# Decode attention with a 48-KB place for the second half of each head's values, and transposes one chunk ahead of the scores

## The chip, the cores and the metric

One core of a Trainium2 chip. The time is that of one execution on the device in microseconds; a kernel is run several times and the median is quoted. The profile is of one execution; its own clock, used in the timelines, starts with the span.

## The reference, cut to what matters

One token passes a pre-norm attention block over a cache and then a small ReLU MLP. There are 32 heads (numbered 0 to 31), a cache of 32768 positions, and 192 values per position and head, all in bf16:

```python
q = (layernorm(x) @ wq)                          # x: 1 x 640, 32 heads of 192
scores = einsum("bhqd,bhkd->bhqk", q, k_cache) * 192 ** -0.5
o = einsum("bhqk,bhkd->bhqd", softmax(scores), v_cache)
h = x + o @ wo
out = h + relu(layernorm(h) @ w1) @ w2           # 640 -> 1536 -> 640
```

Keys and values are 2 x 32 x 32768 x 192 x 2 bytes = 805 MB of the 825 MB that are read. There is one query, so each byte is used once.

## The kernel before

A head is cut into 8 chunks of 32 columns of 128 positions (1 column: one position in each partition). Of each chunk TensorE transposes 20 or 16 columns of keys (line "tp" of the profile), ScalarE copies them out of PSUM ("kT"), TensorE makes their scores ("sp"), and VectorE multiplies and sums the other 12 or 16 columns by itself ("pr", "sc"). ScalarE takes the exponentials of both ("pB", "pA"), and TensorE adds up the values with them ("o_ps"); I call that the value sums of a chunk. The end of a head is a sum of the denominators ("den"), a scaling on VectorE ("o_pair"), a turn of the row into a column on TensorE ("mm<-wide,o_pair") and a copy of it by VectorE ("oT").

GpSimd passes each landing of a load on to the engines (a "relay"), so in the profile a wait "<-POOLq" of TensorE or VectorE is a wait for a load. Keys of half a head are one load of 48-KB rows (K0, K1). Values are four loads of 24-KB rows (V0 to V3) through two places:

```python
    kt = [sbuf(f"kt{i}", [P, JK * Dh], bf16, 512) for i in range(NK)]      # 2 x 48 KB a partition
    vt = [sbuf(f"vt{i}", [P, JL * Dh], bf16, 512) for i in range(NV)]      # 2 x 24 KB
    ...
        for h in range(LAST):                       # the DMA queue, in order; LAST = 31
            keys(h, 0)
            if h > 0:
                vals(h - 1, NL - 1)                 # V3 of the head before
            vals(h, 0)
            keys(h, 1)
            vals(h, 1)
            vals(h, 2)
    ...
    SUMS = ((), (-2,), (-1,), (0, 1), (), (2,), (3,), (4, 5))    # value sums beside chunk c; below 0: of the head before
    def pe_head(g, h, turn=None):
        for c in range(NC):
            transposes(g, h, c)
            ...                                     # den, value sums of SUMS[c]
            scores_pe(g, h, c)
            if c == 3 and h > 0:
                o_turn(g, h - 1)
    ...
    def dve_head(g, h):
        for c in range(len(chunks(h))):
            scores_dve(g, h, c)
            if c == 0 and h > 0:
                den_rec(g, h - 1)
            if c == 2 and h > 0:
                o_scale(g, h - 1)
            if c == 3 and h > 0:
                o_turned(g, h - 1)
```

Heads 1 to 30 run in a loop on each engine. Head 31 is written out apart: its keys and values come in smaller loads and its chunks end with small ones, so that little work is left when the last bytes land. Behind it come w1 and w2 and the MLP.

The softmax here doesn't subtract the row's maximum and nothing guards it: scores larger than these inputs give would overflow.

## Time and profile before

| | before |
|---|---|
| median time | 1920.2 us (3 runs, 1919.48 to 1921.22) |
| span of the profile | 1918.7 us |
| share of the DMA queue's packets | 99.8% |
| VectorE, TensorE busy | 81%, 81% |
| last byte of w2 (packet records) | 1913.6 us |
| output's store issued | 1915.3 us |

The DMA engines are the bound: 39 of the 40 slices show 9 and the last one 8. The prediction shows the lines for it. To them I add those of the end, which it did not look at. They are from the timeline of before (start, length, engine, line, operation, and in brackets the idle time just before it and what ended that):

```profile
start us, us, engine line op out<-in xcount [idle before <-releaser]
...
1821.54 2.56 DVE L688 TENSOR_TENSOR pr<-kt,qb 128x2304 f32<-128x2304 bf16 x1 [2.48 <-POOLq L325]
...
1842.41 3.35 DVE L691 TENSOR_REDUCE sc<-pr 128x16 f32<-128x3072 f32 x1
...
1847.60 2.56 DVE L688 TENSOR_TENSOR pr<-kt,qb 128x2304 f32<-128x2304 bf16 x1 [1.84 <-ACT qb L630]
...
1895.51 1.75 DVE L691 TENSOR_REDUCE sc<-pr 128x8 f32<-128x1536 f32 x1
...
1913.09 1.24 PE L368 MATMUL attT<-h1T,w_s 128*128 128x1 bf16 x30 [0.52 <-DMA w_s<-in_B_w_dram]
...
1915.30 0.36 SPq L230 DMA_DIRECT2D out_dram<-y_row  x1
```

VectorE waits for the second half of head 30's keys until 1821.5 us, ends that head at 1845.8, begins head 31 at 1847.6 and ends its last scores at 1897.3. The MLP's second product waits 0.52 us for w2, so the end hangs on the bytes, but only just: the compute behind head 31 arrives half a microsecond ahead of them.

### The profile page before, as it was taken

The page shows a single profiled execution, that of the slowest core. Times are in us where ns is not written, and L with a number is a line of the kernel's source. Part 1 is how long each engine was busy: PE and PEld are TensorE (multiplying, and loading weights), DVE is VectorE, ACT ScalarE, POOL GpSimd, SP SyncE. Part 2 cuts the span into 40 slices and gives each one's busy share as a digit, 9 for nine tenths or more (in the row PEclk, how much of TensorE's full clock was granted, in tenths as well). Part 3 has the DMA queues.
Part 4 walks back from the last instruction along what each step waited for, and adds up shares of the span by engine and source line. Part 5 has one row for each costly group of instructions (what it writes and reads, how often), then busy time and mean ns, then how long its engine had stood idle before and what let it go on. Part 6 is the DMA issues. An engine that isn't in the chain of part 4 may idle for free.

```text
span 1918.7 us, 36168 instructions
## 1 busy us (share of the span) xinstructions
PE 1560.2 (81%) x15909; PEld 1099.7 (57%) x15909; DVE 1560.0 (81%) x732; ACT 957.9 (50%) x2000; POOL 1.0 (0%) x6
## 2 busy tenths in 40 slices
PE   7787787887877978878878778778788787887887
PEld 7555565555555655655555556556555565565554
DVE  2897787887878978888888879878788787897895
ACT  2554454454554544544545545445445454454463
POOL 0000000000000000000000000000000000000000
PEclk9888888878888878789898888888798888878899
DMA  9999999999999999999999999999999999999998
GB/s 409 429 430 429 432 437 428 434 436 429 436 436 429 435 431 431 438 429 434 436 430 437 433 429 435 430 434 438 428 434 437 427 440 430 431 438 428 434 430 355
DMA packets 34098, 825.29 MB, mean 430 GB/s; under 512 B 3611, under 2 KB 5148, under 8 KB 8604
## 3 DMA queue, kind: packets, MB, share of 16 engines
q1 hardware_dynamic: 34074, 824.98, 99.8%
q8 instruction: 15, 0.25, 0.0%
q14 instruction: 7, 0.06, 0.0%
q10 hardware_dynamic: 2, 0.00, 0.0%
HBM read 824.97 MB, written 0.00 MB: 430 GB/s over the span
## 4 chain that ended last, share of the span: by engine, by line
DMA 55%; PE 30%; DVE 8%; ACT 5%; SPq 1%; issue 1%; POOLq 0%; DVEq 0%; ACTq 0%
DMA kt<-in_A_k_cache_dram 52%; PE o_ps L368 17%; PE tp L387 9%; ACT kT L608 5%; DVE pr L688 4%; DVE sc L691 4%; PE sp L368 3%; DMA vt<-in_A_v_cache_dram 2%; SPq L230 1%; DMA w_s<-in_B_w_dram 1%; PE attT L368 1%; PE mm L368 0%; DMA kt<-in_A_wq_dram 0%; DVEq L65 0%; POOLq L350 0%
## 5 line engine op out<-in xcount | busy, mean ns | idle before, releaser
L688 DVE TENSOR_TENSOR pr<-kt,qb 128x2304 f32<-128x2304 bf16 (+2 forms) x257 | 755.9, 2941 | 299.4 <-POOLq L325 271.2
L608 ACT COPY kT<-tp 128x1024 bf16<-128x1024 bf16 (+1 forms) x899 | 817.7, 989 | 301.2 <-PE tp L387 299.4
L387 PE MATMUL tp<-ident_f,kt 128*128 128x128 f32 x3459 | 580.3, 335 | 238.5 <-POOLq L350 235.7
L691 DVE TENSOR_REDUCE sc<-pr 128x12 f32<-128x2304 f32 (+2 forms) x257 | 755.3, 2939 | 8.9
L387 PEld LDWEIGHTS tp<-ident_f,kt 128*128 128x128 f32 x3459 | 505.2, 175 | 245.6 <-POOLq L350 241.0
L368 PE MATMUL o_ps<-vt,pB 128*2 128x384 bf16 x2286 | 461.9, 352 | 9.0 <-POOLq L350 8.3
L614 ACT ACTIVATE pB<-sp 128x20 bf16<-128x20 f32 (+2 forms) x258 | 48.0, 186 | 569.4 <-PE sp L368 569.4
L368 PE MATMUL o_ps<-vt,pA 128*2 128x384 bf16 x1778 | 330.6, 326 | 0.0
L368 PEld LDWEIGHTS o_ps<-vt,pB 128*2 128x2 bf16 x2286 | 188.0, 88 | 235.5 <-issue 94.5
L368 PE MATMUL sp<-qm,kT 128*128 128x2 bf16 x6918 | 214.3, 164 | 98.4 <-ACT kT L608 96.9
L368 PEld LDWEIGHTS sp<-qm,kT 128*128 128x128 bf16 x6918 | 192.4, 98 | 177.7 <-ACT kT L608 134.5
L368 PEld LDWEIGHTS o_ps<-vt,pA 128*2 128x2 bf16 x1778 | 150.0, 84 | 142.4 <-issue 4.1
L623 ACT ACTIVATE pA<-sc 128x12 bf16<-128x12 f32 (+2 forms) x257 | 53.5, 208 | 39.9 <-DVEq L65 38.9
L614 ACT ACTIVATION_READ_ACCUMULATOR pB<-sp 128x1 f32 x258 | 50.2, 195 | 0.0
L623 ACT ACTIVATION_READ_ACCUMULATOR pA<-sc 128x1 f32 x257 | 48.9, 190 | 0.0
L702 DVE TENSOR_SCALAR o_pair<-o_ps,rec 2x384 bf16<-2x384 f32 x32 | 19.4, 605 | 6.3 <-PE o_ps L368 1.7
L368 PE MATMUL o_ps<-xn_ln,kt 128*96 128x1 bf16 (+1 forms) x316 | 22.4, 208 | 2.6 <-DMA kt<-in_A_wq_dram 2.6
L368 PEld LDWEIGHTS o_ps<-xn_ln,kt 128*96 128x96 bf16 (+1 forms) x316 | 22.2, 175 | 2.7 <-issue 2.6
L368 PE MATMUL attT<-oT,wo_s 128*128 128x1 bf16 x465 | 16.3, 164 | 0.3 <-DVE oT L712 0.3
L712 DVE TENSOR_SCALAR oT<-mm,odd 128x3 bf16<-128x3 f32 x32 | 7.1, 223 | 10.8 <-PE mm L368 8.3
L368 PEld LDWEIGHTS mm<-dsums,ones_mat 128*128 128x128 f32 x64 | 15.4, 295 | 0.3 <-issue 0.3
L696 DVE TENSOR_REDUCE rec<-mm 128x1 f32<-128x20 f32 x32 | 5.7, 179 | 12.0 <-PE mm L368 7.5
(69 smaller groups left out, 151.6 us busy)
## 6 DMA issues: line engine op xcount, KB each, us to landing
vt<-in_A_v_cache_dram SPq DMA_DIRECT2D x126, 3072.0 KB, 19.1
kt<-in_A_k_cache_dram SPq DMA_DIRECT2D x62, 6144.0 KB, 32.6
kt<-in_A_k_cache_dram SPq DMA_DIRECT2D x3, 3072.0 KB, 20.2
wo_s<-in_A_wo_dram SPq DMA_DIRECT2D x16, 480.0 KB, 9.5
kt<-in_A_wq_dram SPq DMA_DIRECT2D x4, 1536.0 KB, 10.8
vt<-in_A_v_cache_dram SPq DMA_DIRECT2D x2, 1536.0 KB, 16.4
kt<-in_A_k_cache_dram SPq DMA_DIRECT2D x1, 1920.0 KB, 28.3
kt<-in_A_v_cache_dram SPq DMA_DIRECT2D x2, 960.0 KB, 21.1
```

The lines of the kernel that those rows point to most:

```text
L230: g.do(lambda: nc.sync.dma_start(out=dst, in_=src), sem, label, by=16)
L368: return lambda: pe.matmul(o, lhsT=w, rhs=r, **kw)
L387: calls.append(lambda b=b, o=o: pe.transpose(out=dst[:, b, :], in_=src[:, o:o + 2 * P].bitcast(f32), identity=ident_f[:]))
L608: g.do(lambda: act.copy(out=kT[c % 2][:, b0:b0 + nb, :], in_=src[:, 0:nb, :].bitcast(bf16)), "act_pe", ("cp", h, c, k))
L614: g.do(lambda: act.activation(out=pB[c % NB][:, 0:jp], in_=sp[:, 0:jp], func=F.Exp, scale=SCALE, accum_out=dsums[:, 2 * c + 1:2 * c + 2]), ...
L623: g.do(lambda: act.activation(out=pA[c % NB][:, 0:jd], in_=sc[c % NC][:, 0:jd], func=F.Exp, scale=SCALE, accum_out=dsums[:, 2 * c:2 * c + ...
L688: g.chain(lambda: dve.tensor_tensor(out=pr[:, 0:j1 - j0, :], in0=src[:, (off + j0) * Dh:(off + j1) * Dh].rearrange("p (j d) -> p j d", d=D ...
L691: g.chain(lambda: dve.reduce_sum(out=sc[c % NC][:, j0:j1], in_=pr[:, 0:j1 - j0, :], axis=X), "dve")
L696: g.chain(lambda: dve.reduce_sum(out=rec[:, 0:1], in_=mm[:, 0:2 * NCM], axis=X), "dve")
L702: g.do(lambda: dve.tensor_scalar_mul(out=o_pair[:, :, 1, :], in0=o_ps[0:2, 0:2 * Dh].rearrange("q (i d) -> q i d", i=2), scalar1=rec[0:2, ...
L712: g.do(lambda: dve.tensor_scalar_mul(out=oT[:], in0=mm[:, 0:3], scalar1=odd[:]), "dve_pe", ("oTc", h))
```

## The change

The intent: fewer and longer rows on a DMA queue that is always full, and a head that ends within itself. The diff, cut to its core (left out: names of semaphores, asserts, the matching order of the relays, places for all 8 chunks' exponentials instead of 5, and ScalarE's order, which now copies a chunk's keys before it takes the exponentials of the chunk before):

```diff
-    vt = [sbuf(f"vt{i}", [P, JL * Dh], bf16, 512) for i in range(NV)]
+    va = sbuf("va", [P, JK * Dh], bf16, 512)          # 48 KB: second half
+    vb = sbuf("vb", [P, JL * Dh], bf16, 512)          # 24 KB: first half, twice
...
-    w2_s = sbuf("w2_s", [P, FT, D], bf16, 512)
+    w2_s = kt[0][:, JL * Dh:JL * Dh + FT * D].rearrange("p (f n) -> p f n", n=D)
...
         for h in range(LAST):
             keys(h, 0)
-            if h > 0:
-                vals(h - 1, NL - 1)
             vals(h, 0)
             keys(h, 1)
-            vals(h, 1)
-            vals(h, 2)
+            for ld in ((2, 1) if h == 0 else (1, 2)):
+                vals(h, ld)                           # 2 is the whole second half
...                                                   # head 31: K0, K1, V0, K2, V1, ... (was K0, V3 of 30, K1, V0, K2, V1, ...)
-    SUMS = ((), (-2,), (-1,), (0, 1), (), (2,), (3,), (4, 5))
+    SUMS = ((), (), (0,), (1,), (), (), (2, 3), (4,), (5, 6, 7))
+    SUMS_0 = ((), (), (0,), (1,), (), (), (4,), (5,), (6, 7, 2, 3))
...
-        for c in range(NC):
-            transposes(g, h, c)
+        for c in range(NC + 1):
+            if c < NC and c != 4:
+                transposes(g, h, c)
...
-            scores_pe(g, h, c)
-            if c == 3 and h > 0:
+            if c > 0:
+                scores_pe(g, h, c - 1)
+            if c == 4:
+                transposes(g, h, 4)
+            if c == 2 and h > 0:
                 o_turn(g, h - 1)
...                                                   # head 31 on TensorE
+        transposes(g, h, 2)
+        values(g, h, 0)
         scores_pe(g, h, 1)
-        ...
+        o_turn(g, h - 1)
...                                                   # VectorE, all heads
             if c == 0 and h > 0:
                 den_rec(g, h - 1)
-            if c == 2 and h > 0:
                 o_scale(g, h - 1)
-            if c == 3 and h > 0:
+            if c == 1 and h > 0:
                 o_turned(g, h - 1)
```

More of the change, by code (lines that the diff above doesn't have):

```diff
@@ L114 @@
     NC = 2 * NL
-    NV = 2
-    NB = 5
+    NB = NC
     LAST = H - 1
     assert Sk % (P * JK) == 0 and NK == 2 and NL == 4 and 2 * Dh == 3 * P and H % 2 == 0 and HE == 3 * P // 4 and DT == 5 and H >= 4
-    full = [(c // 4, (c % 4) * J, J, JPS[c % 2], c // 2, (c % 2) * J) for c in range(NC)]
+    full = [(c // 4, (c % 4) * J, J, JPS[c % 2]) + ((c // 2, (c % 2) * J) if c < 4 else (2, (c - 4) * J)) for c in range(NC)]
     ENDJ = (40, 16, 8)
@@ L198 @@
     mm = psum("mm", [P, 512])
-    wq_c = [kt[1][:, c * H * Dh:(c + 1) * H * Dh] for c in range(DT - 1)] + [vt[1][:, 0:H * Dh]]
+    wq_c = [kt[1][:, c * H * Dh:(c + 1) * H * Dh] for c in range(DT - 1)] + [va[:, 0:H * Dh]]
     assert (DT - 1) * H * Dh == JK * Dh and H * Dh <= JL * Dh
@@ L205 @@
             3: kt[1][:, 64 * Dh:104 * Dh], 4: kt[1][:, 104 * Dh:120 * Dh], 5: kt[1][:, 120 * Dh:128 * Dh]}
-    v_at = {3: kt[0][:, 0:40 * Dh], 4: kt[0][:, 40 * Dh:56 * Dh], 5: kt[0][:, 56 * Dh:64 * Dh]}
-    w1_s = kt[0][:, 64 * Dh:64 * Dh + DT * Dff].rearrange("p (c n) -> p c n", n=Dff)
-    w2_s = sbuf("w2_s", [P, FT, D], bf16, 512)
-    assert DT * Dff <= JL * Dh
+    v_at = {0: vb[:], 1: va[:, 0:JL * Dh], 2: va[:, JL * Dh:2 * JL * Dh],
+            3: vb[:, 0:40 * Dh], 4: vb[:, 40 * Dh:56 * Dh], 5: vb[:, 56 * Dh:64 * Dh]}
+    w1_s = kt[0][:, 0:DT * Dff].rearrange("p (c n) -> p c n", n=Dff)
+    w2_s = kt[0][:, JL * Dh:JL * Dh + FT * D].rearrange("p (f n) -> p f n", n=D)
+    assert DT * Dff <= JL * Dh and FT * D <= JL * Dh
     W2_CUTS = (0, FT // 2, FT - 2, FT)
@@ L215, in v_tile @@
     def v_tile(h, ld):
-        return v_at[ld] if h == LAST and ld in v_at else vt[ld % NV][:]
+        return v_at[ld] if h == LAST else (vb, vb, va)[ld][:]
     names = ["pool_pe", "act_pe", "dve_pe", "act_dve", "dve_act", "dve", "dve_row", "pe_dve", "pool_row", "pool_dve", "pool_act", "pe_act", "pe", "dve_sp"]
-    names += [f"dk{i}" for i in range(NK)] + [f"dv{i}" for i in range(NV)] + ["dwo", "dx", "dout"] + [f"dwq{i}" for i in range(5)]
-    names += [f"dke{i}" for i in range(4)] + ["dvh"] + [f"dve{i}" for i in range(4)] + ["dw1"] + [f"dw2_{i}" for i in range(3)]
+    names += [f"dk{i}" for i in range(NK)] + ["dva", "dvb"] + ["dwo", "dx", "dout"] + [f"dwq{i}" for i in range(5)]
+    names += [f"dke{i}" for i in range(4)] + ["dvh0", "dvh1"] + [f"dve{i}" for i in range(4)] + ["dw1"] + [f"dw2_{i}" for i in range(3)]
     sems = {n: nc.alloc_semaphore(n) for n in names}
@@ L236, in keys @@
             if h > 0:
-                g.wait("PV", h - 1, 2 if h == 1 and ld == 0 else 4 * ld + 1)
+                if ld == 0:
+                    g.wait("PV", h - 1, 4 if h == 1 else 2)
+                else:
+                    g.wait("PV", h - 1, 5)
                 g.wait("scs", h - 1, 4 * ld + 3)
@@ L243, in vals @@
         def vals(h, ld):
-            if ld == 1 and h == LAST:
-                g.wait("vfree")
-            elif ld == 1 and h > 0:
-                g.wait("PV", h, 0)
-            elif ld > 1:
-                g.wait("PV", h, 2 * ld - 3)
-            elif h > 0:
-                g.wait("PV", h - 1, 5)
-            if h < LAST:
-                src = rows(v_hd, h, P * JK * (ld // 2), JK)[:, (ld % 2) * JL * Dh:(ld % 2 + 1) * JL * Dh]
-            else:
-                src = rows(v_hd, h, P * JL * ld, JL)
-            load(vt[ld % NV][:], src, f"dv{ld % NV}", "v", h, ld)
+            if ld == 1:
+                g.wait("PV", h, 1)
+            elif h > 0:
+                g.wait("PV", h - 1, 3 if ld == 0 else NC - 1)
+            src = rows(v_hd, h, P * JK * (ld // 2), JK)
+            if ld < 2:
+                src = src[:, ld * JL * Dh:(ld + 1) * JL * Dh]
+            load((vb, vb, va)[ld][:], src, "dva" if ld == 2 else "dvb", "v", h, ld)
         for c in range(DT):
@@ L275, in end_keys, with end_values @@
             load(k_at[i], rows(k_hd, LAST, k0, jl), sem, "k", LAST, i)
-        for ld in range(NL - 1):
-            if ld != 1:
-                g.wait("PV", LAST - 1, 2 * ld + 1)
-                g.wait("scs", LAST - 1, 2 * ld + 3)
-            end_keys(ld, P * JL * ld, JL, ("dk0", "dke0", "dk1")[ld])
-            if ld == 0:
-                vals(LAST - 1, NL - 1)
-            else:
-                vals(LAST, ld - 1)
+        def end_values(ld, c0, c1, sem, *label):
+            load(v_at[ld][:, c0:c1], rows(v_hd, LAST, P * JL * ld, JL)[:, c0:c1], sem, *label)
+        g.wait("PV", LAST - 1, 2)
+        g.wait("scs", LAST - 1, 3)
+        end_keys(0, 0, JL, "dk0")
+        end_keys(1, P * JL, JL, "dke0")
+        g.wait("PV", LAST - 1, 3)
+        end_values(0, 0, JL * Dh, "dvb", "v", LAST, 0)
+        g.wait("PV", LAST - 1, 5)
+        g.wait("scs", LAST - 1, NC - 1)
+        end_keys(2, 2 * P * JL, JL, "dk1")
+        g.wait("PV", LAST - 1, NC - 1)
+        end_values(1, 0, JL * Dh, "dva", "v", LAST, 1)
         k0 = P * JL * (NL - 1)
@@ L292, in dma_program @@
             k0 += P * jl
-        g.wait("PV", LAST, 1)
-        src = rows(v_hd, LAST, P * JL * (NL - 2), JL)
-        n = J * Dh
-        load(vt[0][:, 0:n], src[:, 0:n], "dv0", "v", LAST, NL - 2)
-        load(vt[0][:, n:2 * n], src[:, n:2 * n], "dvh", "vh")
+        for i in range(2):
+            end_values(2, i * J * Dh, (i + 1) * J * Dh, f"dvh{i}", "vh", i)
         i = 0
@@ L329, in pool_program @@
             key(h, 0)
-            if h > 0:
-                relay(g, "v", h - 1, NL - 1)
             relay(g, "v", h, 0)
             key(h, 1)
-            relay(g, "v", h, 1)
-            relay(g, "v", h, 2)
+            for ld in ((2, 1) if h == 0 else (1, 2)):
+                relay(g, "v", h, ld)
             relay(g, "W", h)
-        for ld in range(NL - 1):
-            key(LAST, ld)
-            if ld == 0:
-                relay(g, "v", LAST - 1, NL - 1)
-            else:
-                relay(g, "v", LAST, ld - 1)
-        relay(g, "v", LAST, NL - 2)
+        key(LAST, 0)
+        key(LAST, 1)
+        relay(g, "v", LAST, 0)
+        key(LAST, 2)
+        relay(g, "v", LAST, 1)
     def relay(g, *label):
@@ L426, in values @@
             g.wait("vc", h, c)
+        elif h == LAST and ld == 2:
+            g.wait("vh", c - 4)
         elif off == 0:
             g.wait("at", "v", h, ld)
-        if h == LAST and c == 5:
-            g.wait("vh")
         g.wait("ep", h, c)
@@ L444, in values @@
                               stop=(c == len(chunks(h)) - 1 and i == len(order) - 1), skip_group_check=True))
-        pe_group(g, calls, ("PV", h, c), "pe_dve" if h < LAST and c == NC - 1 else "pe")
+        pe_group(g, calls, ("PV", h, c), "pe")
     def den_mm(g, h):
@@ L500, in q_spread @@
         pe_group(g, calls, ("qs", h), "pe_act")
-    SUMS = ((), (-2,), (-1,), (0, 1), (), (2,), (3,), (4, 5))
+    SUMS = ((), (), (0,), (1,), (), (), (2, 3), (4,), (5, 6, 7))
+    SUMS_0 = ((), (), (0,), (1,), (), (), (4,), (5,), (6, 7, 2, 3))
     def pe_head(g, h, turn=None):
-        for c in range(NC):
-            transposes(g, h, c)
+        for c in range(NC + 1):
+            if c < NC and c != 4:
+                transposes(g, h, c)
             if c == 0 and h > 0:
                 den_mm(g, h - 1)
-            for d in (SUMS[c] if h > 0 or c > 5 else ((), (0,), (1,), (), (2,), ())[c]):
-                if d >= 0:
+            for d in (SUMS if h > 0 else SUMS_0)[c]:
+                if c < NC:
                     values(g, h, d)
-                elif h > 0:
-                    values(g, h - 1, NC + d)
-            scores_pe(g, h, c)
-            if c == 3 and h > 0:
+            if c > 0:
[3 more added lines that the diff above has]
+            if c == 2 and h > 0:
                 o_turn(g, h - 1)
@@ L521, in pe_head @@
                 q_spread(g, h + 1, turn)
+        for d in (SUMS if h > 0 else SUMS_0)[NC]:
+            values(g, h, d)
     def pe_norm(g):
@@ L546, in pe_end @@
         scores_pe(g, h, 0)
-        values(g, h - 1, NC - 2)
-        values(g, h - 1, NC - 1)
-        pe_group(g, [mmul(attT[0:1, 500:501], ident_b[0:1, 0:1], zero5[0:1, 0:1], start=False, stop=True,
-                          skip_group_check=True)], ("vfree",))
+        transposes(g, h, 2)
+        values(g, h, 0)
         scores_pe(g, h, 1)
-        transposes(g, h, 2)
+        o_turn(g, h - 1)
         transposes(g, h, 3)
+        values(g, h, 1)
         scores_pe(g, h, 2)
-        values(g, h, 0)
+        transposes(g, h, 4)
         scores_pe(g, h, 3)
-        o_turn(g, h - 1)
-        for c in (4, 5):
-            transposes(g, h, c)
-            values(g, h, c - 3)
-            scores_pe(g, h, c)
+        transposes(g, h, 5)
+        values(g, h, 2)
+        scores_pe(g, h, 4)
         transposes(g, h, 6)
         values(g, h, 3)
+        scores_pe(g, h, 5)
         transposes(g, h, 7)
@@ L646, in act_head @@
         q_wide(g, h)
-        for c in range(NC if h < LAST else NC - 2):
-            copies(g, h, c)
-            exp_pe(g, h, c)
-            exp_dve(g, h, c)
+        n = len(chunks(h))
+        for c in range(n):
+            if c == 4 and h < LAST:
+                exp_pe(g, h, 3)
+                exp_dve(g, h, 3)
+                copies(g, h, 4)
+                continue
+            copies(g, h, c)
+            if c > 0:
+                exp_pe(g, h, c - 1)
+                exp_dve(g, h, c - 1)
+        exp_pe(g, h, n - 1)
+        exp_dve(g, h, n - 1)
     def act_end(g):
         act_head(g, LAST)
-        h = LAST
-        copies(g, h, NC - 2)
-        for c in range(NC - 1, NCM):
-            copies(g, h, c)
-            exp_pe(g, h, c - 1)
-            exp_dve(g, h, c - 1)
-        exp_pe(g, h, NCM - 1)
-        exp_dve(g, h, NCM - 1)
         act_norm(g, "ln2")
@@ L699, in o_scale @@
     def o_scale(g, h):
-        g.wait("PV", h, len(chunks(h)) - 1)
+        if h == LAST:
+            g.wait("PV", h, NCM - 1)
         g.wait("rec", h)
```

## The prediction

> **What bounds the kernel now.** I read the page from the top: engine shares, slices, DMA queues.
>
> ```profile
> span 1918.7 us, 36168 instructions
> PE 1560.2 (81%) x15909; PEld 1099.7 (57%) x15909; DVE 1560.0 (81%) x732; ACT 957.9 (50%) x2000; POOL 1.0 (0%) x6
> ...
> DMA  9999999999999999999999999999999999999998
> ...
> DMA packets 34098, 825.29 MB, mean 430 GB/s; under 512 B 3611, under 2 KB 5148, under 8 KB 8604
> ...
> q1 hardware_dynamic: 34074, 824.98, 99.8%
> ```
>
> The 16 DMA engines have no hole in any slice and one queue fills 99.8% of the span, while TensorE and VectorE idle for a fifth of it. 825 MB must be read whatever the order. Next, the busy time by window over the middle of the run, and the DMA queue's own waits:
>
> ```profile
> core 0: us, PE busy (x) PEld busy (x) DVE busy (x) ACT busy (x) POOL busy (x), PEclk, DMA share, GB/s
> ...
> 600.00:1800.00 1200.00, 977.55 (x9887) 687.77 (x9886) 994.39 (x450) 607.77 (x1270) 0.00 (x0) 0.84 1.00 433
> ```
>
> ```profile
> engine line waited for: us in total, times, longest us
> SPq L230 <- PE o_ps L368: 1593.1, 126, 28.0
> ```
>
> The DMA share is 1.00. The issuing queue waits nearly always, and for TensorE's value sums (o_ps) that free a buffer. Such a wait costs nothing while an earlier load still moves. So the kernel is bound by moving bytes, and the question is twofold: does the change make the bytes move faster, and does any of its new waits let the engines run dry.
>
> **How fast a packet moves.** The page counts one packet per row, so a 24-KB row is one packet and a 48-KB row is one. Their durations in the trace's packet records hardly vary: 1280 B 55 ns, 3072 B 121, 12288 B 460, 24576 B 912 (16512 packets), 49152 B 1815 (7936 packets), a semaphore's 4 B 9. From the two large sizes: 1815 - 912 = 903 ns for 24576 B, so 912 - 903 = 9 ns are fixed per packet, and the 4-B packet agrees.
>
> **The Trainium skill.** "DMA: Bandwidth & Descriptors", section "Where 436 GB/s comes from", puts the ceiling of the core's ports at 435.2 GB/s; the trace has 433, so a large gain is not to be had. The same page, "Why small descriptors are slow (HBM only)", names a fixed overhead of about 3 cycles per packet; the trace agrees that there is one, and I use its 9 ns. The same page, "Latency and other measured facts", gives some 600 ns to the first byte; the one load here that met a drying queue was issued at 115.6 us and its first packet started at 117.0, so I use 1.35 us. "TensorE: Matmul & The Clock Gate", "The HAM clock gate", has TensorE at half clock after an idle window of about 3.4 us; the trace agrees: fifteen transposes take 1.84 us, or 3.46 after a wait.
>
> **The change part by part.**
>
> 1. Packets. In each of 31 heads two value loads of 128 24-KB rows become one of 128 48-KB rows: 128 packets fewer, and 16 semaphore packets. (128 + 16) x 9 ns / 16 engines = 0.081 us a head, 2.5 us in all. DMA is the bound, so all of it is on the path. It is the only thing that shortens the work.
>
> 2. Buffers. Before, two 24-KB places took four loads in turn. After, both loads of the first half go through one 24-KB place (vb), and the second half has its own 48-KB place. The order becomes K0, V0, K1, V1, V23. Of the new waits the dangerous one is V1's: it overwrites V0, so it is issued only when chunk 1's sums are done, and behind V0 only K1 is queued. These are the lines of the timeline of before that bear on it (start, length):
>
> ```profile
> start us, us, engine line op out<-in xcount [idle before <-releaser]
> ...
> 1205.70 2.59 PE L387 MATMUL tp<-ident_f,kt 128*128 128x128 f32 x15 [3.76 <-POOLq L350]
> 1205.76 2.56 DVE L688 TENSOR_TENSOR pr<-kt,qb 128x2304 f32<-128x2304 bf16 x1 [4.84 <-POOLq L325]
> 1206.39 3.55 ACT L608 COPY kT<-tp 128x1024 bf16<-128x1024 bf16 x4 [3.63 <-PE tp L387]
> ...
> 1227.19 2.93 SPq L230 DMA_DIRECT2D vt<-in_A_v_cache_dram  x2
> ...
> 1234.69 3.46 PE L387 MATMUL tp<-ident_f,kt 128*128 128x128 f32 x15 [3.99 <-POOLq L350]
> ```
>
> TensorE starts 0.1 us after a K half lands and works through four chunks; the two issues at 1227.19 follow the sums of chunks 0 and 1.
>
> *Deadline.* Count from K0's landing. V0 takes 8 packets an engine, 7.30 us, K1 14.53, so K1 lands at 21.8. Data end 0.6 us before the semaphore (127.88 and 128.50 on the trace's clock), and an issue needs 1.35 us. V1 must be issued by 21.8 - 0.6 - 1.35 = 19.9 for the engine that is last; the first engine runs some 2.6 us ahead (first and last increments of a landing), so it may idle a little from 17.3 on, at no cost to the last.
>
> *When it is issued.* In the trace of before chunk 1's sums end 24.2 us after K0's landing in 17 of 29 heads, at worst 25.7. That path holds two sums of the previous head (2.8 us each) and chunk 2's scores (0.9), which the new order takes out: 24.2 - 6.5 = 17.7, and waits shrink too. Forward: transposes 0 until 2.6 and the den matmul until 2.8, transposes 1 until 5.6 (cold), scores 0 until 6.5, transposes 2 until 8.3, sums 0 until 11.1 (V0 landed at 7.3, ScalarE's exponentials ready at 7.8), scores 1 11.8, the turn 12.1, transposes 3 13.5, sums 1 16.3. VectorE does not hold it up: 5.1 + about 1.0 of small work + 6.7 = 12.8 for chunk 1. So the issue falls at 16.4 to 17.7, 2 to 3.5 us ahead of the deadline.
>
> 3. The second half. VectorE finishes chunk 3 at about 25.2 and ScalarE waits for it before it copies chunk 4, so this half lags K1's landing by 4 us. V1 lands at 29.1, sums 2 and 3 run at 32 to 38: K0 of the next head is issued about 35 while V23 moves until 43.7. V23 lands at 43.7, then sums 4, scores 6 and 7, sums 5, 6, 7: 4 x 2.8 + 0.9 + 0.8 + 0.5 = 57.1, and the next K0 lands at 58.2. TensorE just fits. VectorE (47.3 + 1.5 = 49) and ScalarE (about 30) have room. K1 is issued at 51.6, with K0 and V0 queued until 65.
>
> 4. The first head, once. There V23 goes ahead of V1, and sums 2 and 3 come last. V23 lands at 74.0, chunk 7's VectorE work ends at 37.6 + 47.3 = 84.9, and sums 6, 7, 2, 3 finish at about 96.0. Only then is head 1's V0 issued, while its K0 lands at 82.5 + 14.5 = 97.0: first packet 97.4, data end 96.4. A hole of about 1 us in the last engine: +1.2 with the slow first packet. The kernel before had its own hole in head 1 (0.3 us by the packet records), which goes.
>
> 5. The end. The last loads stand in the same byte order except that head 30's last values come earlier. w2 now goes where keys lay, with the wait that w1 has already. The tail after the last byte is the same work: 0.
>
> Sum: 1920.2 - 2.5 + 1.2 - 0.3 = 1918.6 us.
>
> **The rivals.**
>
> *V1 starves the queue in each head.* If sums 1 came at 21 instead of 17, each of 30 heads would lose 1 us: 1949; at 22 to 23, 1980 to 2010. For it: one place for two loads, a deadline of 19.9. Against it: the path of before, shortened by work that is known to be removed.
>
> *TensorE becomes the bound.* 57.1 of 58.2 us is tight, and cold stretches add 1 to 1.5 us. Lateness goes into the next head's V1, which has 2 to 3.5 us to give, and does not add up while DMA sets the pace. If it used all up: 1930 to 1960.
>
> *Nothing at all.* If the packet's 9 ns were hidden by the next one's start: 1921. The mean rates of the two sizes (430.8 and 433.0 GB/s at 16 engines) speak against it.
>
> *A clear gain* has no room: 98% of the time would need 439 GB/s.
>
> **Range and chances.** Without holes the result is within 2 us of 1918.6; the early hole and how far the engines drift apart are the uncertainty. A starvation of a few tenths in some heads would add up to 8. So 1915.8 to 1926. Faster by over 2%: 0.01. Slower by over 2% needs over 1.2 us lost in each head: 0.05.
>
> **What would show it.** Packets about 4,460 fewer (31 x 144), near 29,640; the 48-KB value loads beside the 24-KB ones; DMA still 9 in each slice and 1.00 in the middle at 433 or 434 GB/s; K0 landing to V1's issue 16 to 18 us; no gap in the packets but one near 96 us. Wrong would be: DMA share under 1.00 in the middle, V1's issue 20 us or more after K0's landing, or TensorE's idle time ahead of a head's first transposes gone and K halves waiting for it.

## The result, and the profile after

| | before | after |
|---|---|---|
| median time | 1920.41 us (4 runs, 1919.48 to 1921.22) | 1927.76 us (4 runs, 1927.38 to 1928.00) |
| DMA packets | 34098 | 29634 |
| last byte of w2 (packet records) | 1913.6 us | 1912.9 us |
| VectorE's last scores end | 1897.3 us | 1907.8 us |
| output's store issued | 1915.3 us | 1922.7 us |

The ratio is 1.0038 (95% interval 1.0021 to 1.0056): the same within 2%, but slower by 7.4 us, and outside the predicted range.

The page of after, the lines that answer to those of before:

```profile
span 1926.1 us, 36134 instructions
PE 1551.9 (81%) x15908; PEld 1088.7 (57%) x15908; DVE 1560.0 (81%) x732; ACT 940.4 (49%) x2000; POOL 1.0 (0%) x6
DMA  9999999999999999999999999999999999999997
DMA packets 29634, 825.29 MB, mean 428 GB/s; under 512 B 3115, under 2 KB 4652, under 8 KB 8108
q1 hardware_dynamic: 29610, 824.98, 99.3%
```

Busy times are nearly the same. Only the last slice differs: 7 instead of 8. The windows of after put the loss at the two ends:

```profile
core 0: us, PE busy (x) PEld busy (x) DVE busy (x) ACT busy (x) POOL busy (x), PEclk, DMA share, GB/s
90.00:110.00 20.00, 16.23 (x144) 10.15 (x143) 11.95 (x7) 10.09 (x15) 0.00 (x0) 1.00 0.94 388
150.00:1800.00 1650.00, 1338.33 (x13572) 936.04 (x13570) 1362.72 (x616) 818.03 (x1742) 0.00 (x0) 0.87 1.00 433
1912.00:1926.00 14.00, 8.45 (x165) 6.03 (x163) 2.71 (x15) 0.57 (x2) 0.00 (x0) 0.72 0.02 6
```

From 150 to 1800 us the DMA share is 1.00 at 433 GB/s, exactly as before. Around 100 us there is a hole (0.94, 388 GB/s; the same window of before has 1.04 and 445: a window counts every packet that starts in it whole, so a share can pass 1). And the last 14 us move next to nothing (0.02): the bytes are there by 1912.9, the compute is not done.

The steady heads went as forecast. One of them in the timeline of after:

```profile
217.63 2.90 PE L383 MATMUL tp<-ident_f,kt 128*128 128x128 f32 x15 [3.02 <-POOLq L346]
...
233.89 0.33 SPq L232 DMA_DIRECT2D vb<-in_A_v_cache_dram  x1
...
239.38 3.19 PE L383 MATMUL tp<-ident_f,kt 128*128 128x128 f32 x15 [3.56 <-POOLq L346]
```

V1 is issued 16.3 us after K0's first transposes (16.4 to 17.7 forecast), and K1's transposes begin 21.8 us after them (21.8 forecast). In heads 2 to 30 the issue comes 16.35 to 16.6 us after the last engine's part of K0 has landed, in head 1 17.2. Nothing runs dry.

The end is another matter. The chain that ended last, in order of time, in after:

```profile
1838.84 27.64 DMA vb<-in_A_v_cache_dram
...
1866.58 4.44 PE o_ps L364 x16
1871.02 0.69 PE sp L364 x24
1871.70 0.26 PE mm L364 x6
1871.99 0.22 DVE oT L713
1872.21 0.16 DVE o_pair L715
...
1872.47 2.57 DVE pr L688
1875.07 2.56 DVE sc L691
...
1913.09 2.06 PE o_ps L364 x12
```

and the lines of its timeline that say why VectorE stood:

```profile
1826.18 2.56 DVE L688 TENSOR_TENSOR pr<-kt,qb 128x2304 f32<-128x2304 bf16 x1 [0.25 <-DVE sc L691]
...
1847.04 3.35 DVE L691 TENSOR_REDUCE sc<-pr 128x16 f32<-128x3072 f32 x1
...
1850.79 0.32 ACT L629 CAST qb<-mm 128x192 bf16<-128x192 f32 x1
...
1852.07 2.56 DVE L688 TENSOR_TENSOR pr<-kt,qb 128x2304 f32<-128x2304 bf16 x1 [1.68 <-POOLq L325]
...
1866.58 3.08 PE L364 MATMUL o_ps<-vb,pB 128*2 128x384 bf16 x10 [2.86 <-POOLq L346]
...
1871.99 0.22 DVE L713 TENSOR_SCALAR oT<-mm,odd 128x3 bf16<-128x3 f32 x1 [5.86 <-PE mm L364]
...
1906.09 1.75 DVE L691 TENSOR_REDUCE sc<-pr 128x8 f32<-128x1536 f32 x1
...
1922.73 0.36 SPq L232 DMA_DIRECT2D out_dram<-y_row  x1
```

Read from the fourth line on (the first three are taken up under "Why the prediction was wrong"): in head 31 the value sums of chunk 0 wait for V0 (2.86 us), which in this head lies behind two key loads: by the landing records it is there 14.6 us after the head's first keys, where a steady head has it after 7.3. In TensorE's program order the turn of head 30's output, which needs nothing of V0, stands behind these sums. VectorE has the copy of that turn after chunk 1, and stands there for 5.86 us. V0 itself lands only 0.3 us later than in the kernel before (1866.5 and 1866.1), and there too the turn stood behind its sums, until 1870.9; but there VectorE took the turn after chunk 3, at 1873.2, and did not wait. From the turn on VectorE has no idle time but 0.22 us until 1907.8, and everything after hangs on it. In the steady heads V0 is there in time and this wait does not exist: the profile has VectorE waiting for a turn twice in all, 6.2 us together, the second time for head 31's own.

### The profile page after: what moved, and what is told of

The parts are those of the page before. It is cut to its first block, busy times and chain, and to the rows that moved or that the text cites. A ratio compares the mean times of both kernels' runs of the same rounds, so it can differ in the third digit from the quotient of the medians.

```text
span 1926.1 us, 36134 instructions
## 1 busy us (share of the span) xinstructions
PE 1551.9 (81%) x15908; PEld 1088.7 (57%) x15908; DVE 1560.0 (81%) x732; ACT 940.4 (49%) x2000; POOL 1.0 (0%) x6
## 2 busy tenths in 40 slices
DMA packets 29634, 825.29 MB, mean 428 GB/s; under 512 B 3115, under 2 KB 4652, under 8 KB 8108
## 4 chain that ended last, share of the span: by engine, by line
DVE 41%; DMA 38%; PE 15%; ACT 5%; issue 1%; DVEq 0%; POOLq 0%; SPq 0%
DMA kt<-in_A_k_cache_dram 34%; DVE sc L691 19%; DVE pr L688 19%; PE o_ps L364 7%; PE tp L383 6%; ACT kT L607 4%; DMA va<-in_A_v_cache_dram 2%; DMA vb<-in_A_v_cache_dram 1%; PE sp L364 1%; DVE o_pair L703 1%; ACT pA L622 0%; DVE oT L713 0%; DMA kt<-in_A_wq_dram 0%; DVE rec L696 0%; DVE rec L697 0%
## 5 line engine op out<-in xcount | busy, mean ns | idle before, releaser
L383 PE MATMUL tp<-ident_f,kt 128*128 128x128 f32 x3459 | 594.8, 332 | 250.4 <-POOLq L346 171.8
L383 PEld LDWEIGHTS tp<-ident_f,kt 128*128 128x128 f32 x3459 | 488.4, 172 | 306.6 <-POOLq L346 186.6
L364 PE MATMUL o_ps<-va,pB 128*2 128x384 bf16 x1152 | 221.8, 341 | 61.1 <-POOLq L346 60.9
L364 PE MATMUL o_ps<-vb,pB 128*2 128x384 bf16 x1154 | 217.6, 335 | 25.4 <-ACT pA L622 20.9
L364 PEld LDWEIGHTS o_ps<-va,pB 128*2 128x2 bf16 x1152 | 94.2, 86 | 157.8 <-POOLq L346 68.9
L364 PE MATMUL o_ps<-va,pA 128*2 128x384 bf16 x896 | 171.5, 333 | 0.0
L364 PE MATMUL o_ps<-vb,pA 128*2 128x384 bf16 x894 | 167.4, 327 | 0.0
L364 PEld LDWEIGHTS o_ps<-vb,pB 128*2 128x2 bf16 x1154 | 91.1, 85 | 127.9 <-ACT pA L622 26.2
L364 PEld LDWEIGHTS o_ps<-va,pA 128*2 128x2 bf16 x896 | 77.1, 86 | 75.6 <-issue 8.8
L364 PEld LDWEIGHTS o_ps<-vb,pA 128*2 128x2 bf16 x894 | 75.5, 84 | 71.4 <-issue 1.9
```

Source lines behind the costliest of these rows:

```text
L364: return lambda: pe.matmul(o, lhsT=w, rhs=r, **kw)
L383: calls.append(lambda b=b, o=o: pe.transpose(out=dst[:, b, :], in_=src[:, o:o + 2 * P].bitcast(f32), identity=ident_f[:]))
```

## The experiments

My theory after reading the two traces: the 7.4 us are the sum of three things. The bytes arrive sooner by the packets saved, later by a hole in head 1, and the tail behind the last byte grew from 1.7 to 9.9 us because VectorE enters head 31 4.5 us later and stands 5.9 us for the turn. The rivals are in the expectations. All nine runs were correct.

**e1: VectorE takes the turn later in head 31.**

```diff
-            if c == 1 and h > 0:
+            if c == (3 if h == LAST else 1) and h > 0:
                 o_turned(g, h - 1)
```

> Changed kernel with one move: in the last head VectorE takes the turned output of head 30 after chunk 3's scores instead of after chunk 1's. Theory (VectorE stands 5.86 us in the last head at that step, waiting for TensorE, which waits for V0, and is the bound from there to the end): the wait goes, VectorE's last scores end about 5.9 us earlier, and the time falls by about 5.9 us to some 1922. Rival 1 (the end is late because head 31's first keys land 7.5 us later than before, and the wait only fills time that would be idle anyway): within 1 us of 1927.8. Rival 2 (the end is late by the first head's hole and the packet engines' drift): 1927.8.

Measured: 1923.28 us median (1922.29 to 1926.46, 4 runs); the wait for the turn is gone from head 31, VectorE's last scores end at 1902.6 instead of 1907.8, and the store is issued at 1917.2 instead of 1922.7. Two lines of its timeline, chunk 2's product and the copy of the turn, both without idle time before them:

```profile
1866.49 2.56 DVE L688 TENSOR_TENSOR pr<-kt,qb 128x2304 f32<-128x2304 bf16 x1
...
1878.95 0.22 DVE L713 TENSOR_SCALAR oT<-mm,odd 128x3 bf16<-128x3 f32 x1
```

The profiled execution (1922.44) shows the full 5.5 us, the median 4.5. Both rivals fall: the wait was on the path. Two of the four executions were 1.7 and 4.0 us above the others; they have no profile, and their cause stays open.

**e9: the same wait taken away on the other side.** Only TensorE's order in head 31 changes:

```diff
         transposes(g, h, 2)
+        o_turn(g, h - 1)
         values(g, h, 0)
         scores_pe(g, h, 1)
-        o_turn(g, h - 1)
```

> Changed kernel with one move on TensorE instead of VectorE: in the last head the turn of head 30's output, which needs nothing of head 31, is issued ahead of chunk 0's value sums instead of behind chunk 1's scores. VectorE's order is untouched. Theory (VectorE's wait of 5.9 us is TensorE standing in order in front of V0, which lands 7 us later behind two key loads): the wait goes all the same, and the time falls to some 1922 to 1923 as with the move on VectorE. Rival (the move on VectorE helped because its own small work went to a freer place): no change, 1927.8, and the wait of 5.9 us stays.

Measured: 1923.41 us (1922.60 to 1928.34, 4 runs, again one far above the others; on another chip than the other experiments, with before at 1919.73 there). The timeline of this kernel:

```profile
1863.68 0.31 PE L364 MATMUL mm<-wide,o_pair 2*128 2x1 bf16 x6
...
1866.27 0.22 DVE L713 TENSOR_SCALAR oT<-mm,odd 128x3 bf16<-128x3 f32 x1
...
1866.59 3.36 PE L364 MATMUL o_ps<-vb,pB 128*2 128x384 bf16 x10 [2.60 <-POOLq L346]
```

The turn now runs before the wait for V0, VectorE goes on at 1866.3 instead of 1872.0, and no idle time stands before its copy. So the cause of these 5 us is shown from both ends: an instruction that was ready stood in TensorE's order behind one that was not.

**e4: head 0 in the common order.**

```diff
-            for ld in ((2, 1) if h == 0 else (1, 2)):
+            for ld in (1, 2):
...
-                    g.wait("PV", h - 1, 4 if h == 1 else 2)
+                    g.wait("PV", h - 1, 2)
...
-            for d in (SUMS if h > 0 else SUMS_0)[c]:
+            for d in SUMS[c]:
```

> Changed kernel, but head 0 runs in the order of all other heads (V1 ahead of the second half's values, the sums in the common order), which lets head 1's first values be issued earlier. Theory (the hole near 97 us costs about 1.5 us and shifts all that follows): 1926.2, and no idle packet engines near 95 to 100 us. Rival (the hole is made good later, since the end is bound by VectorE and not by DMA): 1927.8.

Measured: 1925.52 us (1924.00 to 1925.84), 2.2 us less than the changed kernel's median and 3.0 less than that of its later runs (after_again, below). The same window of this kernel, where the changed kernel had 0.94 and 388 GB/s:

```profile
90.00:110.00 20.00, 18.00 (x171) 11.78 (x169) 11.74 (x7) 10.36 (x17) 0.00 (x0) 1.00 1.00 427
```

The hole is closed, and the rival (made good later) falls: though the end hangs on VectorE, VectorE follows the landings into head 31 (1850.1 against 1852.1 with the hole), and every landing after the hole is late by it.

**e5: both moves.**

> Both moves together. Theory: the gains add, -5.9 and -1.5, to some 1920.3, as fast as the kernel before within 0.5 us; the tail after the last byte is again near 2 us. Rival (another bound takes over in the last head, for instance TensorE's sums): 1922 to 1925.

Measured: 1920.48 us (1919.65 to 1921.87), ratio to before 1.0002 (0.9986 to 1.0019). The time is as expected, one part is not: the last byte is there at 1910.8 and the store is issued at 1916.0, 5.2 us behind it and not near 2. VectorE's last scores end at 1900.0, still 2.8 us later than before. That is what is left of its late start into head 31 (1850.0, against 1847.6 in the kernel before).

**e7: less for VectorE in head 31, nothing else.**

```diff
-    ends = [(c // 2, (c % 2) * J, J, JPS[c % 2]) for c in range(NC - 2)]
+    ends = [(c // 2, (c % 2) * J, J, JPS[0]) for c in range(NC - 2)]      # TensorE 20, VectorE 12 columns
```

> Changed kernel with only the lighter VectorE share in the last head. Theory: chunk 1's saving is eaten by the wait for the turn, which grows from 5.9 to 7.5 us, chunks 3 and 5 save 1.67 us each behind it: 3.3 us less, 1924.4. Rival (the wait is not what sets VectorE's place, the sum of its work is): 5.0 us less, 1922.8. Rival (TensorE or ScalarE are the bound there): 1927.8.

Measured: 1925.12 us (1923.76 to 1926.87, 6 runs), 3.4 us less than after_again of the same rounds (3.3 expected). The reason inside was only half right: the wait for the turn did not grow to 7.5 us, it was 4.25; the work saved in chunk 1 went in part into a longer wait for the denominators (2.62 instead of 0.93 us). The turn came at 1871.4 us, hardly before the 1872.0 of the changed kernel, but the profiled execution, the fastest of the six, had also entered head 31 0.9 us later (1853.0). Counted from there the turn came 1.5 us sooner (18.4 us against 19.9): with more transposes in front of them the sums of chunk 0 waited for V0 for 0.48 us instead of 2.86, and their first ten matmuls took 1.79 us instead of 3.08, at a granted clock of 1.00 against 0.55. The median speaks for the theory, that work saved ahead of the turn is worth little and work saved behind it its length, but the six runs spread over 3.1 us and the fastest comes within 1 us of the first rival's 1922.8: this run does not decide between the two.

**e6: the two moves and the lighter share together.**

> The turn moved and head 0 in the common order, and in the last head chunks 1, 3 and 5 give VectorE 12 columns of keys instead of 16 (TensorE 20 instead of 16). Theory (what is left of the tail after the two moves, some 3.5 us from w2's landing, is VectorE's late start into the last head, so 5.0 us less work for it brings the end back to the last bytes): 1917.0, and the tail from w2's landing to the output's issue 1.5 us as in the kernel before. Rival (TensorE or ScalarE hold the end): 1919.5 to 1921.

Measured: 1917.93 us (1917.61 to 1918.09, 5 runs); before on the same chip 1919.94 (1919.25 to 1921.15, 8 runs, 7 of them earlier). Two lines of its timeline:

```profile
1895.10 1.75 DVE L691 TENSOR_REDUCE sc<-pr 128x8 f32<-128x1536 f32 x1
...
1912.37 0.36 SPq L232 DMA_DIRECT2D out_dram<-y_row  x1
```

VectorE ends at 1896.9, the last byte is there at 1910.6 and the store is issued 1.7 us later, as before. No execution of the one kernel reaches into the range of the other; the ratio is 0.9989, with an interval (0.9974 to 1.0004) that still holds 1. It is the version I would keep, for 2.0 us of 1920.

**e3 and e8: the second half's values again as two loads of 24-KB rows,** once in the changed kernel and once in e6:

```diff
-            load((vb, vb, va)[ld][:], src, "dva" if ld == 2 else "dvb", "v", h, ld)
+            if ld == 2:
+                n = JL * Dh
+                load(va[:, 0:n], src[:, 0:n], "dva", "vfirst", h)
+                load(va[:, n:2 * n], src[:, n:2 * n], "dva", "v", h, ld)
+            else:
+                load(vb[:], src, "dvb", "v", h, ld)
```

> Changed kernel, but the second half's values are again two loads of 24-KB rows, issued one behind the other into the same 48-KB place. Theory (9 ns a packet on the bound): DMA ends 2.5 us later, the tail follows it only where it waits for data; since the last head's VectorE chain starts with the landing of head 31's keys, the whole time rises by about 2.5 us to 1930.3. Rival (the 9 ns lie hidden beside the next packet): 1927.8.

> As the run before last (turn moved, head 0 in the common order, lighter VectorE share), but the second half's values as two loads of 24-KB rows. Where the end hangs on the last bytes the packets' 9 ns must show in full: 2.5 us more than that run, 1919.5. Rival (hidden): equal to it.

e3 measured 1928.37 us (1927.25 to 1929.85), which lies within the spread of the changed kernel's two sets of runs (1927.38 to 1929.35): inconclusive as a time. Its packet records show the last byte at 1915.4 us, 2.6 us later than in the changed kernel's first profile and 1.9 than in its second. e8 measured 1919.13 us (1918.84 to 1919.57) against 1917.93 of e6 in the same rounds: 1.2 us, with no overlap; the last bytes are 1.6 us apart (1912.2 and 1910.6). So the saving is real, the rival of a hidden cost falls, but only half to all of the 2.5 us worked out from 9 ns a packet arrives at the end. Why not all of it in e8 stays open.

**after_again: the yardstick.**

> The changed kernel itself, as a yardstick on the chip of this call: 1927 to 1928.

Measured: 1928.49 us (1927.71 to 1929.35, 5 runs), slightly above the expected 1927 to 1928; ratio to before 1.0044.

## Why the prediction was wrong

It failed in its step 5, "The tail after the last byte is the same work: 0." The tail measured 8.2 us more. The work is the same, and the step took it that the work would also be ready when the last bytes land. It had worked out the steady head with care and carried it over to head 31, where the order of the loads differs: V0 comes behind two key loads there, and the new place of the turn (after chunk 1) relies on V0 being early: the turn came 19.7 us after the landing of the first keys, where step 2 has it at 12.1 in a steady head. By the profiles, step by step, with the forecast against the measured:

| step | forecast | measured |
|---|---|---|
| 1. packets | -2.5 us | -1.2 us of time (e6 against e8), -1.6 to -2.6 us of last byte (e8, e3) |
| 2. V1's issue after K0's landing | 16.4 to 17.7 us, no hole | 16.3 us, none |
| 3. second half | fits, no hole | fits: share 1.00 at 433 GB/s |
| 4. hole in head 1 | +1.2, and -0.3 for the old one | +2.2 to +3.0 us of time (e4) |
| 5. tail behind the last byte | 0 | +8.2 us (1.7 to 9.9) |

The last byte itself came 0.7 us earlier than before, where -1.6 was forecast: the packets' saving and the hole nearly cancel. With the tail that makes 8.16 - 0.73 = 7.4 us, the whole difference of the two profiles. How the 0.7 us come about is not shown: in the profile of after_again the last byte is as late as before (1913.5), and by the mean of the 16 engines the last load lands 0.5 us later than before (1912.1 and 1911.6); only the engines' spread is smaller there, 2.2 us instead of 4.0.

Of the tail, 5.9 us are the wait for the turn; e1 and e9 took it away in two ways and brought 5.2 and 5.1 us against the median of after_again, or 4.5 and 4.4 against that of the changed kernel's first set.

The rest is VectorE's start into head 31 at 1852.1 instead of 1847.6. What released it was the landing of the keys after, and ScalarE's copy of the query ("qb") before. But that landing held it for little: VectorE itself ended head 30 only at 1850.4 (1845.8 before), and the query was there only at 1851.1, so keys that came earlier would have gained at most 1 us (1852.1 less 1851.1). The lateness comes from head 30. Its first keys land 7.5 us later (1799.95 and 1792.44), as a head's V3 now moves ahead of the next head's keys, and VectorE then works through both halves without a wait for keys between them: it begins the second half at 1826.2, 4.5 us behind K1's landing, where before it waited for K1 until 1821.5. Step 3 had this number ("this half lags K1's landing by 4 us") and did not carry it into the end. No run undid the order of the loads; that the start makes up the rest is read from the traces, and e5, e6 and e7 agree with it.

The wait and the late start together make VectorE's last scores 10.6 us later (1907.8 and 1897.3), and not all of that reaches the store: from VectorE's end to the last value sum it took 9.5 us before and 7.3 after, and from there to the store 8.6 and 7.6, since before the sums and then w2 were waited for or still in work. So the kernel before had some 3 us of slack behind VectorE, and the changed one used it up first.

The rivals of the prediction did not come: V1 starved nothing, TensorE did not become the bound. None of them looked at head 31, so none names what happened.

The mechanism named under "no gap but one near 96 us" was right, its size was not: I let the last of the 16 engines lose 1 us, while landings behind the hole are late by about 2 us (the last engine's part of head 1's V0 lands 9.2 us after that of K0, where its packets take 7.3). By the packet records the 16 engines stood idle for 1.5 us on average from 80 to 150 us (0.03 before), and their first packets after the hole took 0.9 to 2.3 us, 1.6 on average, instead of 0.91.

## What to carry to other kernels

A DMA share of 1.00 through the middle says that the middle is bound by bytes; it says nothing about the first and last heads, so work out the chain behind the last landings of its own whenever the order of loads or of instructions changes. The Trainium skill's "Perfetto Trace Analysis", section "Optimization Strategy", speaks of kernels with several regimes in which the bound changes over time; this case has three, and the changed one lost in the two short ones. When a small step moves to an earlier place in an in-order engine, look at what stands in front of it in every copy of the loop body, the written-out last one too: here one ready instruction behind one late load cost more than all the packets saved.

## What the Trainium skill lacked or had wrong

- "DMA: Bandwidth & Descriptors", "Why small descriptors are slow (HBM only)": it gives a per-packet overhead of about 3 cycles and finds joining descriptors worth it only at 256 B or less. Here some 8 to 9 ns a packet are fixed from 1280 B to 48 KB (55, 912 and 1815 ns for 1280 B, 24 KB and 48 KB), and halving the number of already long packets in a quarter of the traffic was still worth 1.2 us of 1919.
- The same page, "Latency and other measured facts": about 600 ns to the first byte on this path. The first load of the run started its first packet 1.03 us after its issue, the load behind the hole in head 1 of the changed kernel 0.96 us, and a load issued in the kernel before while the queue ran dry 1.35 us; that last one's first packet took 1208 ns instead of 912.
- No page says how far the 16 engines drift apart: the first and the last of them finish one load 1.8 to 2.7 us apart in the steady heads of these runs, so a hole is not one number for a load.
